# A range check moved behind the last eviction of its expert's first product, in twelve pieces over six experts

## The chip, the cores and the metric

One of the cores of a Trainium2 chip runs the whole kernel. A time is the microseconds that the chip takes for one execution. The kernel before took 680.99 us, the median of three runs (678.45 to 681.20).

The engines of the core work side by side, each through a queue of its own, in the order of that queue: TensorE (PE in the profile, its weight loads PEld) multiplies matrices into PSUM; VectorE (DVE), ScalarE (ACT) and GpSimd (POOL) work on tiles, GpSimd not on PSUM; SyncE (SP) issues most of the transfers. An instruction waits on semaphores until what it needs is there, and what stands behind it in its engine's queue waits with it.

## The reference

A gated recurrence feeds a mixture of experts. For every one of 4 x 8 heads and 768 steps of time, with complex gates a = a_re + i a_im of 48 channels:

```python
mag = np.sqrt(a_re * a_re + a_im * a_im)
scale = np.minimum(mag, 0.999) / (mag + 1e-06)
S = (a * scale)[..., None] * S + k[..., :, None] * v[..., None, :]     # complex state, 48 x 48
y = q @ S.real
```

The rows of all heads of a token, 384 numbers, are then x of 3072 tokens. Each token goes to the one of 8 experts that has its greatest logit:

```python
expert_idx = np.argmax(x @ w_gate, axis=1)
h = np.maximum(x_sorted[lo:hi] @ w1[e], 0.0)      # 384 -> 1024
y_sorted[lo:hi] = h @ w2[e]                       # 1024 -> 384
out = gate_w[:, None] * y[inv_perm]
```

## The kernel before

**Two stages.** The first stage (to about 330 us) computes the recurrence in chunks, routes the tokens and scatters their rows into a table in memory, sorted by expert. The second stage runs over the eight experts; the change is in it alone.

**An expert.** Each expert has room for CAP = 448 tokens, three tiles of 128 and one of 64 (expert 0 works in two parts). `gather` fetches its rows one expert ahead. `turn` transposes them on TensorE and copies the three parts of `xt` out of PSUM, the one in the middle on ScalarE (L78). In `expert` the first product goes over f = 0 to 7 (F = 1024 in eight parts): six matmuls a part into `hps`, which has three PSUM buffers, and a Relu into `ht`, on VectorE for even f (L589), on ScalarE for odd f (L587). The second product goes over the four tiles of tokens: 16 matmuls a tile into `yps`, which has two PSUM buffers; VectorE multiplies a full tile by the gate into `y` (L598); the short tile is put together from two halves by a copy on ScalarE (L605) and two operations on VectorE (L606, L607). GpSimd scatters each `y` to the output (L570). The second product reads all eight parts of `ht` for its first tile, and so can't get past the matmuls on f = 0 to 6 before the Relu of f = 7 is there.

**The weights.** `load_w(e + 2)` is written behind expert e: w1 (L162) goes out when the first product of e is over, w2 (L163) when the second is. Both are on SP's queue.

**The range check.** The first stage's method holds only for gates in a certain range. `range_check` therefore goes through all gates once more, in NC = 12 pieces of 128 x 768: it counts in `bad` where |a_im| exceeds 1.5 a_re or the square of the magnitude is under 0.37. A piece has two loads (L624), six operations on ScalarE (L626, L627, L629, L630, L632, L633, the last two with a sum into `bad`) and two on GpSimd (L628, L631), with two buffers for each of its four tiles. ScalarE and GpSimd take turns: the addition needs both Squares, the Copy overwrites what the addition read, the subtraction needs the Copy, the two Relus need the results of GpSimd. `verdict`, written behind expert 6, turns `bad` and the routing's overflow into `flag`: a sum on VectorE (L637 to L641), a matmul `bp`, a copy. If `flag` isn't zero, a slow version runs at the end; with these inputs it doesn't.

**What sets the order.** The text of the program gives priorities, and a planner writes each engine's queue: by a model of its own it simulates the engines, and at each moment takes the earliest written of the operations that it holds to be ready. `queue(ins, before)` ties an instruction behind another in that order, without a wait. The three pieces of each of e = 2 to 5 are written behind `load_w(e + 2)`, and so come to run in the first product of experts 3 to 6; their loads are tied behind the w2 load.

Of the kernel before, what the change touches and what calls it, by code (L numbers as in the profile page):

```python
# [10 lines left out]
FP = mybir.dt.float32  # L11
I32 = mybir.dt.int32
BF = mybir.dt.bfloat16
AF = mybir.ActivationFunctionType
# [6 lines left out]
P = 128  # L21
# [4 lines left out]
SLOPE = 1.5  # L26
# [11 lines left out]
def kernel(  # L38
# [12 lines left out]
    nc = tc.nc  # L51
# [4 lines left out]
    E, _, F = w1.shape  # L56
# [17 lines left out]
    def mm(o, lhsT, rhs, start=True, stop=True):  # L74
        return nc.tensor.matmul(o, lhsT=lhsT, rhs=rhs, start=start, stop=stop, skip_group_check=True)  # L75
# [10 lines left out]
    def const(shape, name, dt=FP):  # L86
        return cp.tile(shape, dt, name=name)
# [57 lines left out]
    T, W_T = {"put": []}, {}  # L145

    def queue(ins, before):

        tc.add_manual_dep(ins.ins, before.ins.name, NOSYNC, reason="queue order")
        return ins  # L150


    def load_w(e, parts=None):

        if e not in W_T:
            W_T[e] = [
                wp[e % 2].tile([P, n, w], FP, tag=nm, name=nm + "t") for nm, n, w in (("w1", KD, F), ("w2", KF, DM))
            ]
        a, b = W_T[e]
        w1e, w2e = w1[e].rearrange("(i p) f -> p i f", p=P), w2[e].rearrange("(i p) d -> p i d", p=P)  # L160
        if parts is None:
            nc.sync.dma_start(out=a, in_=w1e)  # L162
            T["w"] = nc.sync.dma_start(out=b, in_=w2e)  # L163
        else:
            for i in parts:
                o, x, i = (a, w1e, slice(i, i + 1)) if i < KD else (b, w2e, slice(2 * (i - KD), 2 * (i - KD) + 2))
                queue(nc.sync.dma_start(out=o[:, i], in_=x[:, i]), T["ld"])
# [307 lines left out]
    def gather(s, sizes):  # L475

        n = len(sizes)
        xg = gp.tile([P, n, XW], FP, tag="xg", padded_shape=[P, CT, XW], name="xg")
        f = sum(m == P for m in sizes)
        nc.sync.dma_start(out=xg[:, :f], in_=xs[s : s + f * P].rearrange("(i p) c -> p i c", p=P))  # L480
        if f < n:
            nc.sync.dma_start(out=xg[0 : sizes[f], f], in_=xs[s + f * P : s + f * P + sizes[f]])
        return xg
# [3 lines left out]
    for z in range(2):  # L487
        nc.sync.dma_start(
            out=wg[z * DP : z * DP + D, :, 0:E],
            in_=w_gate.rearrange("(i z d) e -> z d i e", z=2, d=D)[z],  # L490
# [59 lines left out]
    ck = ctx.enter_context(tc.tile_pool(name="ck", bufs=2))  # L550
# [4 lines left out]
    def turn(sizes, xg):  # L555
        n, w = len(sizes), sum(sizes)
        xt = xp.tile([P, KD, w], FP, tag="xt", padded_shape=[P, KD, CAP], name="xt")
        for d in range(KD):
            tp = psX.tile([P, w], FP, tag="tp", padded_shape=[P, 512], name="tp")
            for i, m in enumerate(sizes):  # L560
                nc.tensor.transpose(
                    out=tp[:, i * P : i * P + m],
                    in_=xg[0:m, i, d * P : (d + 1) * P],
                    identity=ident[0:m, 0:m],
                )
            copy(d, xt[:, d], tp)
        return xt

    def scatter(y, idx, m):
        return nc.gpsimd.indirect_dma_start(  # L570
            out=out,
            out_offset=bass.IndirectOffsetOnAxis(ap=idx, axis=0),
            in_=y[0:m],
            in_offset=None,
            bounds_check=N - 1,
            oob_is_err=False,
        )

    def expert(sizes, xt, wa, wb, xg):
        w = sum(sizes)  # L580
        ht = hp.tile([P, KF, w], FP, tag="ht", padded_shape=[P, KF, CAP], name="ht")
        for f in range(KF):
            ps = psH.tile([P, w], FP, tag="h", padded_shape=[P, 512], name="hps")
            for d in range(KD):
                mm(ps, wa[:, d, f * P : (f + 1) * P], xt[:, d], d == 0, d == KD - 1)
            if f % 2:
                nc.scalar.activation(out=ht[:, f], in_=ps, func=AF.Relu)  # L587
            else:
                nc.vector.tensor_scalar(out=ht[:, f], in0=ps, scalar1=0.0, scalar2=None, op0=OP.max)  # L589
        for i, m in enumerate(sizes):  # L590
            ps = psO.tile([P, DM], FP, tag="y", padded_shape=[P, 512], name="yps")
            y = yp.tile([P, DM], FP, tag="y", name="y")
            h = ht[:, :, i * P : i * P + m]
            gate = xg[0:m, i, DM : DM + 1]
            if m == P:
                for f in range(KF):
                    mm(ps, h[:, f], wb[:, f], f == 0, f == KF - 1)
                nc.vector.tensor_scalar(out=y, in0=ps, scalar1=gate, scalar2=None, op0=OP.mult)  # L598
            else:

                for f in range(KF // 2):
                    for z in range(2):
                        g = z * (KF // 2) + f
                        mm(ps[z * HT : (z + 1) * HT], h[:, g], wb[:, g], f == 0, f == KF // 2 - 1)
                nc.scalar.copy(out=y[0:m], in_=ps[HT : HT + m])  # L605
                nc.vector.tensor_tensor(out=y[0:m], in0=ps[0:m], in1=y[0:m], op=OP.add)  # L606
                nc.vector.tensor_scalar(out=y[0:m], in0=y[0:m], scalar1=gate, scalar2=None, op0=OP.mult)  # L607
            scatter(y, xg[0:m, i, DM + 1 : DM + 2].bitcast(I32), m)
# [3 lines left out]
    CW = 768  # L612
    NC = B * H * S * D // (P * CW)
    bad = const([P, 2, NC], "bad")
    mag2 = const([P, 1], "mag2")
    nc.vector.memset(mag2, MAG2_MIN)
    flat = [a.rearrange("b h s d -> (b h s d)").rearrange("(p n) -> p n", p=P) for a in (a_re, a_im)]

    def range_check(i):

        ar = ck.tile([P, CW], FP, tag="car", name="car")
        ai = ck.tile([P, CW], FP, tag="cai", name="cai")
        for t, a in zip((ar, ai), flat):
            queue(nc.sync.dma_start(out=t, in_=a[:, i * CW : (i + 1) * CW]), T["w"])  # L624
        s, w = [ck.tile([P, CW], FP, tag=nm, name=nm) for nm in ("cs", "cw")]
        nc.scalar.activation(out=s, in_=ar, func=AF.Square)  # L626
        nc.scalar.activation(out=w, in_=ai, func=AF.Square)  # L627
        nc.gpsimd.tensor_tensor(out=s, in0=s, in1=w, op=OP.add)  # L628
        nc.scalar.activation(out=ai, in_=ai, func=AF.Abs)  # L629
        nc.scalar.activation(out=w, in_=ar, func=AF.Copy, scale=SLOPE)  # L630
        nc.gpsimd.tensor_tensor(out=ai, in0=ai, in1=w, op=OP.subtract)  # L631
        nc.scalar.activation(out=ai, in_=ai, func=AF.Relu, accum_out=bad[:, 0, i : i + 1])  # L632
        nc.scalar.activation(out=s, in_=s, func=AF.Relu, scale=-1.0, bias=mag2, accum_out=bad[:, 1, i : i + 1])  # L633

    def verdict():

        nc.vector.tensor_scalar(out=bad, in0=bad, scalar1=0.0, scalar2=None, op0=OP.is_gt)  # L637
        two = xl.tile([P, 2], FP, tag="two", name="two")
        nc.vector.reduce_sum(two[:, 0:1], bad.rearrange("p a i -> p (a i)"), axis=AX_X)
        nc.vector.reduce_sum(two[:, 1:2], ov, axis=AX_X)  # L640
        nc.vector.tensor_tensor(out=two[:, 1:2], in0=two[:, 1:2], in1=two[:, 0:1], op=OP.add)  # L641
        bp = psX.tile([1, 2], FP, tag="tp", padded_shape=[1, 512], name="bp")
        mm(bp, ones[:, 0:1], two)
        nc.vector.tensor_copy(out=flag, in_=bp)
# [4 lines left out]
    for e in range(E):  # L649
        if e == 0:  # L650
            part = [([P] * (FIRST // P), own0), (rest0, gather(FIRST, rest0))]
        else:
            part = [(own, xg)]
        for i, (sizes, g) in enumerate(part):
            xt = turn(sizes, g)
            if i == len(part) - 1 and e + 1 < E:
                xg = gather((e + 1) * CAP, own)
            expert(sizes, xt, *W_T[e], g)
        if e + 2 < E:
            load_w(e + 2)  # L660
        if e >= 2:
            for i in range(NC):
                if i % (E - 4) == e - 2:
                    range_check(i)
        if e == E - 2:
            verdict()

# [151 lines left out]
```

## Time and profile before

| | |
|---|---|
| median of three runs | 680.99 us (678.45 to 681.20) |
| the profiled execution, its own time | 680.82 us |
| its span, first to last instruction | 678.8 us |
| mean granted clock of TensorE | 0.953 |
| TensorE matmuls busy | 591.6 us, 87% of the span |
| ScalarE busy | 276.0 us, 41% |
| VectorE busy | 238.3 us, 35% |
| GpSimd busy | 215.4 us, 32% |

The span runs from the first to the last instruction; the execution's own time has 2.0 us more around it. The granted clock is the share of full speed that the chip gave TensorE. Busy times of different engines overlap; idle time of an engine counts only where TensorE, or the end, waits for it.

### The profile page before, as it was taken

To read this page: it belongs to the slowest core of one execution; us is meant where nothing else is said; L and a number is where in the kernel's file an instruction comes from. 1 tells how busy PE (TensorE), PEld (TensorE's weight loads), DVE (VectorE), ACT (ScalarE), POOL (GpSimd) and SP (SyncE) were. 2 spreads that over 40 slices of the span, in tenths; PEclk is the share of its full clock that TensorE was granted. 3 is DMA by queue.
4 is the path that set the end of the run, shared out by engine and by line. 5 is a ranking of instruction groups with operands and counts; after the bars stand their busy time and mean duration, and the time that the engine had idled before them with its cause. 6 is when DMAs were issued, how large, how long until landed. Compare 5 with 4: busy or idle time off the path is not lost. (4 is left out here: it accounts for less than half of the span.)

```text
span 678.8 us, 8550 instructions
## 1 busy us (share of the span) xinstructions
PE 591.6 (87%) x3319; PEld 384.1 (57%) x3319; DVE 238.3 (35%) x487; ACT 276.0 (41%) x467; POOL 215.4 (32%) x206
## 2 busy tenths in 40 slices
PE   0497889897898899899999999997997997979993
PEld 0185667675776768677766555553553553535451
DVE  2453557566566547664312112120120210201210
ACT  4655765753863764663201101037054072270100
POOL 3543164254363462442121010125133143151001
PEclk9996799899899789899999999999997998997998
DMA  9999763753752641233126234364183362620000
GB/s 164 225 300 169 111 126 64 155 126 62 152 118 60 130 81 24 63 106 116 48 81 207 68 123 138 116 238 140 38 271 104 121 192 94 228 65 24 8 13 29
DMA packets 151673, 79.74 MB, mean 117 GB/s; under 512 B 130134, under 2 KB 141927, under 8 KB 151624
## 3 DMA queue, kind: packets, MB, share of 16 engines
q1 hardware_dynamic: 143168, 63.75, 39.8%
q0 software_dynamic: 4736, 15.20, 6.5%
q10 hardware_dynamic: 3720, 0.16, 0.3%
q8 instruction: 28, 0.46, 0.3%
q14 instruction: 21, 0.17, 0.1%
HBM read 63.74 MB, written 15.98 MB: 117 GB/s over the span
## 5 line engine op out<-in xcount | busy, mean ns | idle before, releaser
L75 PE MATMUL yps<-w2t,ht 128*128 128x384 f32 (+1 forms) x512 | 158.7, 510 | 17.4 <-ACT ht L587 17.2
L75 PE MATMUL hps<-xt,w1t 128*128 128x448 f32 (+2 forms) x432 | 147.0, 500 | 0.0
L75 PEld LDWEIGHTS yps<-w2t,ht 128*128 128x128 f32 (+1 forms) x512 | 85.3, 186 | 89.1 <-issue 24.2
L75 PEld LDWEIGHTS hps<-xt,w1t 128*128 128x128 f32 x432 | 79.9, 190 | 61.6 <-issue 58.2
L570 POOL DMA_INDIRECT out_dram<-y,xg x32 | 30.8, 961 | 199.7 <-DVE y L598 163.8
L75 PE MATMUL at<-qt,kt 96*128 96x128 f32 x384 | 58.5, 300 | 17.1 <-ACT kt L78 9.3
L75 PEld LDWEIGHTS at<-qt,kt 96*128 96x128 f32 x384 | 51.8, 208 | 28.0 <-ACT kt L78 12.8
L598 DVE TENSOR_SCALAR y<-yps,xg 128x384 f32<-128x384 f32 x24 | 14.8, 617 | 145.2 <-PE yps L75 145.2
L589 DVE TENSOR_SCALAR ht<-hps 128x448 f32<-128x448 f32 (+2 forms) x36 | 20.6, 572 | 102.4 <-PE hps L75 102.4
L605 ACT COPY y<-yps 64x384 f32<-64x384 f32 x8 | 3.8, 476 | 126.3 <-PE yps L75 126.3
L587 ACT ACTIVATE ht<-hps 128x448 f32<-128x448 f32 (+2 forms) x36 | 17.8, 495 | 87.3 <-PE hps L75 87.3
L75 PE MATMUL y<-am,v 128*64 128x128 f32 x384 | 51.0, 299 | 0.0
L320 POOL TENSOR_TENSOR Qe<-q,E 128x384 f32<-128x384 f32 x24 | 23.9, 998 | 84.6 <-ACT E L185 84.5
L424 DVE TENSOR_TENSOR am<-at,tri 128x512 f32<-128x512 f32 x48 | 33.0, 688 | 37.5 <-PE at L75 37.4
L75 PE MATMUL csl<-A,tri_half 128*128 128x384 f32 x48 | 25.4, 616 | 21.1 <-DVE A L238 18.5
L75 PE MATMUL y<-qt,G 96*64 96x128 f32 x320 | 42.2, 281 | 0.0
L391 POOL DMA_INDIRECT xs<-x,to x24 | 24.3, 1013 | 55.9 <-DMA xs<-x,to 36.6
L416 PE MATMUL tp<-ident,Q 128*96 128x128 f32 x192 | 35.0, 304 | 3.7 <-DVE Q L324 3.7
L75 PEld LDWEIGHTS y<-am,v 128*64 128x64 f32 x384 | 31.2, 144 | 10.1 <-issue 6.9
L75 PE MATMUL dk<-v,K 128*96 128x48 f32 x320 | 34.1, 260 | 2.8 <-DVE t L454 2.8
L191 ACT ACT_TABLE_LOAD x27 | 34.6, 1283 | 2.3 <-PEq L805 0.8
L75 PEld LDWEIGHTS dk<-v,K 128*96 128x96 f32 x320 | 32.4, 177 | 5.0 <-DVE t L454 4.0
(124 smaller groups left out, 816.6 us busy)
## 6 DMA issues: line engine op xcount, KB each, us to landing
w1t<-in_moe_w_dram SPq DMA_DIRECT2D x7, 1536.0 KB
w2t<-in_moe_w_dram SPq DMA_DIRECT2D x7, 1536.0 KB
xs<-zrow POOLq DMA_DIRECT2D x1, 5404.0 KB, 23.7
ar<-in_a_re_dram SPq DMA_DIRECT2D x12, 384.0 KB
ai<-in_a_im_dram SPq DMA_DIRECT2D x12, 384.0 KB
q<-in_q_dram SPq DMA_DIRECT2D x12, 384.0 KB
k<-in_k_dram SPq DMA_DIRECT2D x12, 384.0 KB
v<-in_v_dram SPq DMA_DIRECT2D x12, 384.0 KB
```

The lines of the kernel that those rows point to most:

```text
L75: return nc.tensor.matmul(o, lhsT=lhsT, rhs=rhs, start=start, stop=stop, skip_group_check=True)
L191: ins = nc.scalar.preload_act_table_set(name)
L320: T[nm] = nc.gpsimd.tensor_tensor(out=e.rearrange("p h d -> p (h d)"), in0=T[src, u][:, sl], in1=T[dec, u][:, sl], op=OP.mult)
L391: return nc.gpsimd.indirect_dma_start(out=xs[:, :], out_offset=bass.IndirectOffsetOnAxis(ap=to[:, i : i + 1], axis=0), in_=x[:, i], in_off ...
L416: nc.tensor.transpose(out=tp[0:DD, j], in_=X[:, hg * 4 + j], identity=ident)
L424: nc.vector.tensor_tensor(out=am, in0=at, in1=bc(tri, 1, 4), op=OP.mult)
L570: return nc.gpsimd.indirect_dma_start(out=out, out_offset=bass.IndirectOffsetOnAxis(ap=idx, axis=0), in_=y[0:m], in_offset=None, bounds_ch ...
L587: nc.scalar.activation(out=ht[:, f], in_=ps, func=AF.Relu)
L589: nc.vector.tensor_scalar(out=ht[:, f], in0=ps, scalar1=0.0, scalar2=None, op0=OP.max)
L598: nc.vector.tensor_scalar(out=y, in0=ps, scalar1=gate, scalar2=None, op0=OP.mult)
L605: nc.scalar.copy(out=y[0:m], in_=ps[HT : HT + m])
```

## The change

The pieces of the range check are dealt out in pairs to experts 1 to 6, in place of three pieces to each of four. `range_check` is split in two. `range_load` issues a piece's two loads and is written where the check was, at the end of expert e (0 to 5). The operations themselves are handed to the next expert in `beside`, and written between its first and its second product. Every operation on ScalarE is tied in ScalarE's order: the first behind the Relu of f = 7, each behind the one before it, and the Relu of f = 1 of the following expert behind the last of the pair. The last two Relus of a piece have changed places. `verdict` stays where it was.

```diff
-    def expert(sizes, xt, wa, wb, xg):
+    def expert(sizes, xt, wa, wb, xg, beside=()):
...
             if f % 2:
-                nc.scalar.activation(out=ht[:, f], in_=ps, func=AF.Relu)
+                relu = nc.scalar.activation(out=ht[:, f], in_=ps, func=AF.Relu)
+                if T.get("beside"):
+                    queue(relu, T.pop("beside"))
             else:
                 nc.vector.tensor_scalar(out=ht[:, f], in0=ps, scalar1=0.0, scalar2=None, op0=OP.max)
+        for f in beside:
+            relu = T["beside"] = f(relu)
...
-    def range_check(i):
-
-        ar = ck.tile([P, CW], FP, tag="car", name="car")
-        ai = ck.tile([P, CW], FP, tag="cai", name="cai")
-        for t, a in zip((ar, ai), flat):
-            queue(nc.sync.dma_start(out=t, in_=a[:, i * CW : (i + 1) * CW]), T["w"])
+    def range_load(i):
+        t = [ck.tile([P, CW], FP, tag=nm, name=nm) for nm in ("car", "cai")]
+        for o, a in zip(t, flat):
+            queue(nc.sync.dma_start(out=o, in_=a[:, i * CW : (i + 1) * CW]), T["w"])
+        T["ck", i] = t
+
+    def range_check(i, before):
+
+        ar, ai = T.pop(("ck", i))
         s, w = [ck.tile([P, CW], FP, tag=nm, name=nm) for nm in ("cs", "cw")]
-        nc.scalar.activation(out=s, in_=ar, func=AF.Square)
-        nc.scalar.activation(out=w, in_=ai, func=AF.Square)
+
+        def on_act(**kw):
+            nonlocal before
+            before = queue(nc.scalar.activation(**kw), before)
+
+        on_act(out=s, in_=ar, func=AF.Square)
+        on_act(out=w, in_=ai, func=AF.Square)
         nc.gpsimd.tensor_tensor(out=s, in0=s, in1=w, op=OP.add)
-        nc.scalar.activation(out=ai, in_=ai, func=AF.Abs)
-        nc.scalar.activation(out=w, in_=ar, func=AF.Copy, scale=SLOPE)
+        on_act(out=ai, in_=ai, func=AF.Abs)
+        on_act(out=w, in_=ar, func=AF.Copy, scale=SLOPE)
         nc.gpsimd.tensor_tensor(out=ai, in0=ai, in1=w, op=OP.subtract)
-        nc.scalar.activation(out=ai, in_=ai, func=AF.Relu, accum_out=bad[:, 0, i : i + 1])
-        nc.scalar.activation(out=s, in_=s, func=AF.Relu, scale=-1.0, bias=mag2, accum_out=bad[:, 1, i : i + 1])
+        on_act(out=s, in_=s, func=AF.Relu, scale=-1.0, bias=mag2, accum_out=bad[:, 1, i : i + 1])
+        on_act(out=ai, in_=ai, func=AF.Relu, accum_out=bad[:, 0, i : i + 1])
+        return before
...
-            expert(sizes, xt, *W_T[e], g)
+            todo = []
+            if i == len(part) - 1 and 1 <= e < E - 1:
+                todo = [lambda b, i=i: range_check(i, b) for i in range(NC) if i % (E - 2) == e - 1]
+            expert(sizes, xt, *W_T[e], g, todo)
         if e + 2 < E:
             load_w(e + 2)
-        if e >= 2:
-            for i in range(NC):
-                if i % (E - 4) == e - 2:
-                    range_check(i)
+        for i in range(NC):
+            if i % (E - 2) == e:
+                range_load(i)
         if e == E - 2:
             verdict()
```

## Rows read from the trace of the kernel before

**Rows 1.** Waits from 380 to 680 us: total, times, longest.

```profile
PE yps L75 <- ACT ht L587: 17.2, 6, 4.1
```

**Rows 2.** Busy time by stretch: experts 1 and 3 to 6 (us, engines, clock, DMA).

```profile
368.40:407.00 38.60, 38.56 (x126) 20.56 (x124) 6.37 (x11) 3.18 (x6) 3.86 (x4) 1.00 0.35 114
445.61:490.43 44.82, 40.73 (x126) 21.20 (x125) 6.37 (x11) 17.85 (x30) 14.71 (x10) 0.96 0.45 152
490.43:536.79 46.36, 42.13 (x127) 21.89 (x125) 6.37 (x11) 17.85 (x30) 14.69 (x10) 0.93 0.45 147
536.79:582.03 45.24, 40.79 (x126) 21.17 (x125) 6.37 (x11) 17.85 (x30) 14.71 (x10) 0.96 0.45 150
582.03:629.05 47.02, 42.27 (x128) 22.00 (x126) 6.89 (x14) 17.85 (x30) 14.71 (x10) 0.93 0.35 114
```

**Rows 3.** The same: second products of experts 1 and 3, expert 4 after its stop.

```profile
388.70:407.00 18.30, 18.30 (x65) 9.99 (x63) 1.85 (x3) 0.54 (x1) 2.93 (x3) 1.00 0.31 111
465.90:490.43 24.53, 20.47 (x65) 10.63 (x64) 1.85 (x3) 6.69 (x12) 7.02 (x6) 0.93 0.22 83
...
519.86:536.79 16.93, 16.93 (x51) 8.94 (x51) 1.85 (x3) 0.00 (x0) 2.93 (x3) 0.82 0.07 28
```

**Rows 4.** Timeline of TensorE, experts 3 and 4: start, length, what.

```profile
474.91 15.59 PE L75 MATMUL yps<-w2t,ht 128*128 128x384 f32 x50 [4.06 <-ACT ht L587]
...
519.86 16.99 PE L75 MATMUL yps<-w2t,ht 128*128 128x384 f32 x50 [4.05 <-ACT ht L587]
```

**Rows 5.** Timeline of ScalarE in expert 3.

```profile
454.52 0.84 ACT L627 ACTIVATE cw<-cai 128x768 f32<-128x768 f32 x1 [0.28 <-DMA cai<-in_a_im_dram]
...
461.63 0.52 ACT L587 ACTIVATE ht<-hps 128x448 f32<-128x448 f32 x1
...
467.25 0.82 ACT L626 ACTIVATE cs<-car 128x768 f32<-128x768 f32 x1
...
468.72 0.52 ACT L587 ACTIVATE ht<-hps 128x448 f32<-128x448 f32 x1
...
473.49 0.84 ACT L632 ACTIVATE cai<-cai 128x768 f32<-128x768 f32 x1 [0.99 <-POOL cai L631]
...
474.33 0.52 ACT L587 ACTIVATE ht<-hps 128x448 f32<-128x448 f32 x1
```

**Rows 6.** Timeline of ScalarE from expert 1 to expert 2.

```profile
384.39 0.54 ACT L587 ACTIVATE ht<-hps 128x448 f32<-128x448 f32 x1 [3.97 <-PE hps L75]
388.90 0.54 ACT L587 ACTIVATE ht<-hps 128x448 f32<-128x448 f32 x1 [3.97 <-PE hps L75]
407.12 0.48 ACT L605 COPY y<-yps 64x384 f32<-64x384 f32 x1 [17.68 <-PE yps L75]
408.53 0.53 ACT L78 COPY xt<-tp 128x448 f32<-128x448 f32 x1 [0.94 <-PE tp L561]
```

**Rows 7.** Timeline of GpSimd, experts 1 and 3.

```profile
394.95 0.98 POOL L570 DMA_INDIRECT out_dram<-y,xg  x1 [22.15 <-DVE y L598]
400.11 0.98 POOL L570 DMA_INDIRECT out_dram<-y,xg  x1 [4.18 <-DVE y L598]
405.27 0.98 POOL L570 DMA_INDIRECT out_dram<-y,xg  x1 [4.19 <-DVE y L598]
...
468.89 1.82 POOL L628 TENSOR_TENSOR cs<-cs,cw 128x768 f32<-128x768 f32 x1 [2.51 <-ACT cw L627]
471.66 1.80 POOL L631 TENSOR_TENSOR cai<-cai,cw 128x768 f32<-128x768 f32 x1 [0.95 <-ACT cw L630]
```

**Rows 8.** Timeline of SP's queue in expert 3.

```profile
446.19 0.52 SPq L624 DMA_DIRECT2D car<-in_a_re_dram  x1
...
454.53 0.38 SPq L480 DMA_DIRECT2D xg<-xs  x1
```

**Rows 9.** Timeline of VectorE, experts 1 and 6.

```profile
399.22 0.62 DVE L598 TENSOR_SCALAR y<-yps,xg 128x384 f32<-128x384 f32 x1 [4.54 <-PE yps L75]
...
611.54 0.18 DVE L637 TENSOR_SCALAR bad<-bad 128x24 f32<-128x24 f32 x1 [10.65 <-ACT cai L632]
```

## The prediction

> **What bounds the kernel now.** I read the page first: TensorE is by far the busiest engine, so only what makes TensorE idle or slow can be won. Then the waits, cut to the expert stage: the largest wait of TensorE there is on ScalarE's Relu of `ht`, 17.2 us in six waits [rows 1]; the longer waits in that view belong to engines waiting for TensorE. Then busy time by stretch, one stretch for each expert. Experts 1 and 2 take 38.6 us at a granted clock of 1.00, experts 3 to 6 take 44.82, 46.36, 45.24 and 47.02 us at 0.93 to 0.96 [rows 2]. The four that are long are the four with range-check work on ScalarE (17.85 us busy against 3.18) and GpSimd. Their excess over 38.60 is 6.22 + 7.76 + 6.64 + 8.42 = 29.0 us.
>
> Where in an expert is it? The second product alone takes 18.30 us in expert 1 and 24.53 us in expert 3, 6.23 more, which is the whole excess of that expert [rows 3]; the turn and the first product cost nothing extra, even with the checks and their loads beside them. The timelines show the mechanism. In expert 3 TensorE stops for 4.06 us before its 15th matmul of the second product until `ht` comes [rows 4], and `ht` is late because the Relu of f = 7 stands in ScalarE's queue behind the last operation of the third piece: that operation starts at 473.49 us, the Relu at 474.33 us [rows 5], although the first product ended at 465.90 us. [...]
>
> **The change, part by part.** *The order.* The checks now start behind Relu f = 7 of their own expert, so no Relu of the first product can stand behind them. That removes the stops and with them what slows the clock: -29.0 us, if nothing new stands in their place. What hides the checks is the second product: 18.30 us in which ScalarE has one 0.54 us Relu at the start and then nothing until the copy of the short tile at 407.12 us [rows 6].
>
> *Does a pair fit?* One piece in the new order (two Squares, Abs, Copy after the addition, two Relus) took, as piece three of expert 3, from 467.25 us to the next instruction at 474.33 us: 7.08 us, with GpSimd's addition (1.82 us) and subtraction inside it; the Relu that stood within hid in the wait for the addition [rows 5, 7]. The swap of the two last Relus only writes down the order that ScalarE already had. Two pieces are 14.16 us. In expert 1 Relu f = 7 runs from 388.90 to 389.44 us, so the chain ends at about 403.6 us. The first thing behind it on ScalarE is the copy that can't start before 407.12 us: 3.5 us of slack. After that comes the copy of `xt` from 408.53 to 409.06 us, which the next first product waits for. So per expert the cost is nothing, covered by the second product; if the cover were gone, each us over the 3.5 would hold that copy and then TensorE.
>
> The rule that nothing overtakes on ScalarE is what cost the time before: the Relu of f = 7 waited 8 us behind check work [rows 5]. [...]
>
> *GpSimd.* It now has four tensor operations of about 1.81 us between the scatters of the same product [rows 7]. In the piece just shown the addition began 1.64 us after the first Square and the subtraction 4.41 us after it [rows 5, 7]. With the first Square 0.54 us behind the start of Relu f = 7, and counted from that start, ScalarE asks for add 1 at +2.2 us, subtract 1 at +4.95, add 2 at +9.3, subtract 2 at +12.0; the scatters come free at +6.05, +11.21 and +16.37 us (394.95, 400.11, 405.27 us) and take 0.98 us [rows 7]. In that order of time only the second scatter touches the chain: it ends at +12.19, which costs subtract 2 about 0.2 us. The trace of before doesn't show the new order on GpSimd. The bounds: nothing if the order follows the real times; 2.1 to 2.9 us, still within the slack, if the first scatter stands ahead of subtract 1 and the second ahead of add 2. I take nothing. What hints at the order that the planner will choose is the one it chose before: one Relu of the first product (461.63, 468.72 us) to each piece, though in fact a piece takes 7.08 us and the Relus are 4.5 us apart [rows 5, 6]. So it believed a piece to be shorter against TensorE's work than it is, and will put the checks' operations early, ahead of the scatters, which is the harmless side.
>
> *The loads.* They move one expert ahead of their use, still behind w2's load on SP's queue. At expert 3 they were issued from 446.19 us and the first pair had landed by 454.52 us [rows 5, 8]; issued right behind the end of the expert before, as there, a pair has until Relu f = 7, some 20 us after that end. The gather queued behind them comes 8 us after the first of them [rows 8]. There is no third pair any more that waits for a buffer in the middle of an expert; the buffers of a pair are free at 403.6 us, before the w2 load at the expert's end. Expert 3's first product, in which such loads landed, lost nothing (above), so I cost them at zero.
>
> *Experts 1 and 2* now carry a pair too: zero by the same sum.
>
> *The verdict.* It now waits for the second piece of expert 6. Before, `bad` stood in VectorE's queue 10.65 us waiting for its last piece, ahead of the first eviction [rows 9]. If it is planned between the first and second eviction of expert 6, the second (399.22 us in expert 1's times) waits until 403.6 + 0.6 for the verdict's operations and ends at about 404.8; with two `yps` buffers the fourth tile, which starts when the third is done (404.4, 5.16 us behind the second by their scatters), is held some 0.5 us. Planned later it costs nothing; planned ahead of the first eviction, the third tile is held some 6 us, and with the clock loss of the stops above 8 to 10 us. I take 0.5.
>
> **Sum.** Profiled execution 680.8 us (span 678.8 and 2.0 around it; the median of three runs is 681.0, so the same). 680.8 - 29.0 + 0.5 = 652.3 us.
>
> **Rivals.**
> 1. *A chain held on GpSimd, middle size.* If the second scatter (ends +12.19) stands ahead of subtract 1, that ends at +14.0, piece two begins 0.87 us later, as the next instruction did after the subtraction of the piece shown [rows 5, 7], and ScalarE is free at +22.0, 410.9 us. Two copies of 0.5 us later, at 411.9 us, `xt` is there, 2.8 us after the 409.06 of before: 2.8 us in each of six experts, and 2.2 more where the clock falls: 652 + 17 to 30 = 669 to 682 us. For it: the four operations and three scatters do share one queue. Against: the planner's early checks. Chance 0.05.
> 2. *Slower than before.* The same mechanism one scatter further decides: with the third (ends +17.35) ahead of subtract 1, everything is 5.2 us later again, and TensorE loses 8.0 us and 2.2 to 3.7 of clock (what the stops of experts 3 and 4 cost beyond their length) in each of six experts: 61 to 70 us, some 715 us. It turns slower than before when the loss per expert passes 29 / 6 = 4.8 us. Against it: the third scatter comes free 11 us after that subtraction is asked for. Chance 0.03.
> 3. *The change moves the stall, no gain.* If the chain's ends are so late that the next expert's first Relu, tied behind them, is held as f = 7 was, the 29 us come back in another place: 677 to 684 us. With three `hps` buffers the product stops first at f = 4, half its 18 us after it began, which is when the `xt` copy ends at 409.06 us, so ScalarE would have to be late with f = 1 until 418 us, 14 us after the chain's end by my sum. Against: just that distance. Chance 0.04.
> 4. *The verdict ahead of the first eviction*: 652 + 8 to 10 = 660 to 662 us, with smaller mishaps at the seams between 655 and 660. Chance 0.10.
>
> **How the numbers follow.** The forecast has 0.78 and its own range is 650 to 655 us. The three runs shown lie between 678.45 and 681.2, so I let the low end go to 649.5; the high end takes in most of the fourth rival, to 660. Left out are the rest of rival 4 and rivals 1 to 3, under 2 in 10. Half a per cent, 3.4 us, is about what a measurement of this kernel can tell from no change. Faster: the forecast, rival 4 and most of rival 1, 0.92; same: rival 3 and the top of rival 1, 0.04; slower: rival 2 and a rest, 0.04.
>
> **What would show it.** Right: experts 1 to 6 each within 0.3 us of 38.6 us and at clock 1.00; no wait of TensorE for ScalarE's `ht`; six chains that each begin within 0.6 us of a Relu of f = 7, the pair about 14.2 us later; the copy of the short tile following TensorE at once, and the scatters within a microsecond of their evictions. Wrong: a gap before the first product on the copy of `xt`, GpSimd's tensor operations waiting behind scatters, a range-check load still on its way when the chain begins, or `bad` holding an eviction for more than a tile.

## The result, and the profile after

The changed kernel takes 651.35 us (median of four runs, 650.07 to 655.58) against 679.72 us for the kernel before (four runs, 675.53 to 681.20): a ratio of 0.9603, 95% interval 0.9539 to 0.9667. The forecast was 652.3 us in a range of 649.5 to 660. The profiled execution took 650.52 us, its span is 648.5 us.

Busy time by stretch, one row for each of experts 1 to 7, as in [rows 2] (us of the stretch; busy time and instructions of TensorE, its weight loads, VectorE, ScalarE, GpSimd; granted clock; DMA share; GB/s):

```profile
367.18:405.79 38.61, 38.58 (x127) 20.56 (x125) 6.38 (x11) 13.19 (x22) 10.99 (x8) 1.00 0.45 153
405.79:444.38 38.59, 38.55 (x126) 20.56 (x124) 6.38 (x11) 13.19 (x22) 11.09 (x9) 1.00 0.45 157
444.38:482.99 38.61, 38.58 (x127) 20.57 (x125) 6.38 (x11) 13.19 (x22) 11.12 (x9) 1.00 0.46 156
482.99:521.58 38.59, 38.55 (x126) 20.56 (x124) 6.38 (x11) 13.19 (x22) 11.11 (x9) 1.00 0.45 156
521.58:560.19 38.61, 38.58 (x127) 20.57 (x125) 6.38 (x11) 13.18 (x22) 11.10 (x9) 1.00 0.44 156
560.19:599.25 39.06, 38.74 (x128) 20.64 (x126) 6.62 (x14) 13.19 (x22) 10.28 (x8) 1.00 0.33 115
599.25:637.90 38.65, 38.03 (x124) 20.55 (x124) 6.53 (x12) 3.18 (x6) 4.80 (x5) 1.00 0.04 15
```

Experts 1 to 5 each take 38.6 us at a clock of 1.00, though ScalarE now works 13.2 us in each of them. Only expert 6, with the verdict, is 0.46 us longer. Against [rows 2] experts 3 to 6 give back 6.21 + 7.77 + 6.63 + 7.96 = 28.6 us. The rest of the difference between the two profiled executions, 30.3 us, is 1.2 us ahead of expert 1, which begins at 367.18 us instead of 368.40 behind the first stage and expert 0, whose work the change doesn't touch, and 0.5 us behind expert 6.

ScalarE in expert 1, its timeline around the pair (start, length, what, idle time ahead of it and what ended that):

```profile
387.68 0.54 ACT L588 ACTIVATE ht<-hps 128x448 f32<-128x448 f32 x1 [3.97 <-PE hps L75]
388.12 0.83 ACT L637 ACTIVATE cs<-car 128x768 f32<-128x768 f32 x1
...
395.22 0.83 ACT L637 ACTIVATE cs<-car 128x768 f32<-128x768 f32 x1
...
402.21 0.19 ACT L637 ACTIVATION_READ_ACCUMULATOR cai<-cai 128x1 f32 x1
405.90 0.47 ACT L610 COPY y<-yps 64x384 f32<-64x384 f32 x1 [3.50 <-PE yps L75]
407.25 0.53 ACT L78 COPY xt<-tp 128x448 f32<-128x448 f32 x1 [0.88 <-PE tp L561]
```

The answer to [rows 6]: the Relu of f = 7 starts when TensorE has finished its product, the first piece follows 0.44 us later, the second 7.10 us after that, and the pair ends at 402.40 us. Then ScalarE is idle 3.50 us until TensorE ends: the slack of the forecast, 3.5 us.

GpSimd in expert 1, its timeline:

```profile
389.77 1.81 POOL L641 TENSOR_TENSOR cs<-cs,cw 128x768 f32<-128x768 f32 x1 [18.18 <-ACT cw L637]
392.53 1.81 POOL L644 TENSOR_TENSOR cai<-cai,cw 128x768 f32<-128x768 f32 x1 [0.95 <-ACT cw L637]
394.49 1.00 POOL L570 DMA_INDIRECT out_dram<-y,xg  x1 [0.15 <-issue]
396.87 1.80 POOL L641 TENSOR_TENSOR cs<-cs,cw 128x768 f32<-128x768 f32 x1 [1.38 <-ACT cw L637]
399.62 1.81 POOL L644 TENSOR_TENSOR cai<-cai,cw 128x768 f32<-128x768 f32 x1 [0.95 <-ACT cw L637]
401.59 0.99 POOL L570 DMA_INDIRECT out_dram<-y,xg  x1 [0.16 <-issue]
```

All six pairs show this order: the first two scatters of an expert each stand behind a subtraction, and no scatter stands ahead of an operation of the pair that was wanted at that time. The second scatter is 3 us late, its `y` having been ready at 398.62 us; nothing waits for it.

At the verdict, VectorE and TensorE in expert 6 (two timelines):

```profile
595.43 0.18 DVE L651 TENSOR_SCALAR bad<-bad 128x24 f32<-128x24 f32 x1 [8.97 <-ACT cai L637]
595.64 0.18 DVE L653 TENSOR_REDUCE two<-bad 128x1 f32<-128x24 f32 x1
595.74 0.61 DVE L603 TENSOR_SCALAR y<-yps,xg 128x384 f32<-128x384 f32 x1
...
596.40 2.80 PE L75 MATMUL yps<-w2t,ht 128*64 128x384 f32 x16 [0.28 <-DVE y L603]
```

`bad` stands between the first and the second eviction of expert 6 and holds the second until 595.74 us; TensorE stops 0.28 us before its last tile.

### The profile page after: what moved, and what is told of

Read it like the earlier page. It is cut to its first block, busy times and chain, and to the rows that moved or that the text cites. A ratio compares the mean times of both kernels' runs of the same rounds, so it can differ in the third digit from the quotient of the medians.

```text
span 648.5 us, 8554 instructions
## 1 busy us (share of the span) xinstructions
PE 577.9 (89%) x3319; PEld 378.7 (58%) x3319; DVE 238.3 (37%) x487; ACT 277.8 (43%) x467; POOL 215.0 (33%) x206
## 5 line engine op out<-in xcount | busy, mean ns | idle before, releaser
L75 PE MATMUL yps<-w2t,ht 128*128 128x384 f32 (+1 forms) x512 | 147.2, 488 | 0.3 <-DVE y L603 0.3
L75 PEld LDWEIGHTS yps<-w2t,ht 128*128 128x128 f32 (+1 forms) x512 | 81.4, 177 | 64.5 <-issue 15.0
L75 PE MATMUL at<-qt,kt 96*128 96x128 f32 x384 | 57.1, 295 | 18.1 <-ACT qt L78 9.4
L75 PEld LDWEIGHTS at<-qt,kt 96*128 96x128 f32 x384 | 50.3, 203 | 28.8 <-ACT qt L78 12.9
L641 POOL TENSOR_TENSOR cs<-cs,cw 128x768 f32<-128x768 f32 x12 | 21.6, 1804 | 117.4 <-ACT cw L637 117.4
L75 PE MATMUL y<-am,v 128*64 128x128 f32 x384 | 49.1, 288 | 0.0
L78 ACT COPY qt<-tp 96x512 f32<-96x512 f32 x48 | 27.0, 581 | 20.1 <-PE tp L416 18.8
```

The costliest lines, as they stand in the source:

```text
L78: (nc.scalar.copy if i % 2 else nc.vector.tensor_copy)(out=o, in_=in_)
```

## Experiments

Totals of these kernels also hold the first stage and expert 0, whose code none of them touches and which took 364.6 to 371.5 us in their profiled executions. So the table gives two things: all runs, and in the profiled execution the time from the start of expert 1's transposes to the end of the span.

| kernel | median us | ratio to before (95%) | span less start of expert 1, us |
|---|---|---|---|
| before | 679.72 | 1 | 678.8 - 368.40 = 310.4 |
| changed | 651.35 | 0.960 (0.954 to 0.967) | 648.5 - 367.18 = 281.3 |
| spread alone | 649.97 | 0.958 (0.950 to 0.967) | 647.4 - 365.95 = 281.5 |
| place alone | 667.17 | 0.985 (0.978 to 0.993) | 662.7 - 365.80 = 296.9 |
| no tie | 651.66 | 0.962 (0.954 to 0.970) | 650.1 - 368.98 = 281.1 |
| no check | 654.53 | 0.962 (0.952 to 0.971) | 653.0 - 371.51 = 281.5 |
| four a time | 685.32 | 1.012 (1.006 to 1.019) | 683.1 - 368.36 = 314.7 |
| subtractions behind a scatter | 673.32 | 0.992 (0.988 to 0.996) | 671.6 - 366.85 = 304.8 |
| two, then one | 648.35 | 0.958 (0.954 to 0.962) | 645.8 - 364.61 = 281.2 |
| verdict later | 651.65 | 0.961 (0.955 to 0.966) | 649.2 - 367.87 = 281.3 |

The ratios are to the runs of the kernel before on the same chip as each kernel; the medians of the first two rows are those given above.

**1. The dealing alone.** The forecast took the new place for what removes the stops. The first run, an edit of the kernel before, does without it.

```diff
-        if e >= 2:
-            for i in range(NC):
-                if i % (E - 4) == e - 2:
-                    range_check(i)
+        for i in range(NC):
+            if i % (E - 2) == e:
+                range_check(i)
```

> The kernel before with one edit: a pair of pieces to each of experts 1 to 6 in place of three pieces to each of four; nothing is tied, loads and operations stay where they were written, so the checks run in the first product. Theory: what cost 29 us was the third piece, since only Relu f = 7 behind it came too late; with two pieces of 7.1 us from some 5 us into the first product on, Relu f = 7 can follow less than 2 us after its product, and the second product needs it only some 4.6 us after that product's end. So 651 to 653 us, no wait of TensorE for ht. Rival (the place behind f = 7 and the tie make the gain): Relus f = 5 and f = 7 are still held behind check work, TensorE still stops, now in six experts, and the time is over 660 us.

Measured: 649.97 us, and 281.5 us from expert 1 on: the whole gain. ScalarE in expert 3, its timeline:

```profile
450.99 0.84 ACT L626 ACTIVATE cs<-car 128x768 f32<-128x768 f32 x1 [0.33 <-DMA car<-in_a_re_dram]
...
459.32 0.52 ACT L587 ACTIVATE ht<-hps 128x448 f32<-128x448 f32 x1
...
464.10 0.84 ACT L632 ACTIVATE cai<-cai 128x768 f32<-128x768 f32 x1 [1.00 <-POOL cai L631]
464.85 0.19 ACT L632 ACTIVATION_READ_ACCUMULATOR cai<-cai 128x1 f32 x1
464.94 0.95 ACT L587 ACTIVATE ht<-hps 128x448 f32<-128x448 f32 x2
```

The pair runs in the middle of the first product and holds the Relus of f = 3 and f = 5, the latter until 464.94 us. Both last Relus are then done at 465.89 us, 2.4 us after the second product began at 463.45 us, and TensorE's rows show no stop. In [rows 5] the Relu of f = 7 started 8.4 us after that point. What cost the time before was the third piece ahead of it.

**2. The place alone.** The changed kernel with three pieces to each of experts 3 to 6.

```diff
-        t = [ck.tile([P, CW], FP, tag=nm, name=nm) for nm in ("car", "cai")]
+        t = [ck.tile([P, CW], FP, tag=nm, name=nm, bufs=3) for nm in ("car", "cai")]
...
-        s, w = [ck.tile([P, CW], FP, tag=nm, name=nm) for nm in ("cs", "cw")]
+        s, w = [ck.tile([P, CW], FP, tag=nm, name=nm, bufs=1) for nm in ("cs", "cw")]
...
-            if i == len(part) - 1 and 1 <= e < E - 1:
-                todo = [lambda b, i=i: range_check(i, b) for i in range(NC) if i % (E - 2) == e - 1]
+            if i == len(part) - 1 and 3 <= e < E - 1:
+                todo = [lambda b, i=i: range_check(i, b) for i in range(NC) if i % (E - 4) == e - 3]
...
-            if i % (E - 2) == e:
+            if i % (E - 4) == e - 2:
                 range_load(i)
```

> The changed kernel with the old dealing: three pieces to each of experts 3 to 6, loaded one expert ahead (three buffers for each of the two loaded tiles, one for each of the two others so that they fit), tied behind Relu f = 7 as in the change. Theory: the chain is 21.3 us where some 17.8 are free, so the copy of the short tile is some 3.5 us late and the middle part of xt some 2.6 us; TensorE waits 1.8 to 2.6 us at the start of four first products, plus up to 2.2 us each where the clock falls: 651 + 7 to 19 = 658 to 670 us. Rival (the place alone makes the gain, the number of pieces doesn't matter): 650 to 653 us.

Measured: 667.17 us, 15.6 us more from expert 1 on than the change (296.9 - 281.3). ScalarE, then TensorE, at the seam from expert 3 to expert 4 (two timelines):

```profile
485.14 0.19 ACT L637 ACTIVATION_READ_ACCUMULATOR cai<-cai 128x1 f32 x1
485.35 0.48 ACT L610 COPY y<-yps 64x384 f32<-64x384 f32 x1
485.86 0.53 ACT L78 COPY xt<-tp 128x448 f32<-128x448 f32 x1
...
486.44 17.56 PE L75 MATMUL hps<-xt,w1t 128*128 128x448 f32 x46 [1.67 <-ACT xt L78]
```

The chain takes 21.4 us (463.93 to 485.33 us) and ends 3.7 us after the second product; the two copies follow without a gap, and the first product of expert 4 stops 1.67 us before its third matmul. Three seams have that stop; at the last, after expert 6, the verdict's matmul waits 4.42 us for VectorE's sums, which wait for the last piece. These waits are 9.4 of the 15.6 us. Most of the rest is TensorE's own pace: behind the second of the three stops the first product goes on for 18.95 us at a granted 0.92, behind the other two for 17.39 us at 1.00, and the 48 matmuls of expert 7's first product take 20.83 us instead of 18.14.

**3. Without the tie.** The changed kernel, all else as it is.

```diff
-                if T.get("beside"):
-                    queue(relu, T.pop("beside"))
...
-            before = queue(nc.scalar.activation(**kw), before)
+            before = nc.scalar.activation(**kw)
```

> The changed kernel without the ties in ScalarE's order; loads one expert ahead, operations written at the same place between the products, pairs over six experts. The planner then mixes the checks into the first product, with Relu f = 7 behind the pair's last operation. Theory: a pair begun behind f = 1 and held up by f = 3 and f = 5 still ends some 1.5 us after the first product, Relu f = 7 comes some 3 us before it is needed, no stop: 650 to 653 us, as the change. Rival (the tie is what makes the gain): stops of TensorE on ht come back in six experts, 655 us or more.

Measured: 651.66 us, 281.1 us from expert 1 on. The planner does move the checks into the first product. ScalarE, then TensorE, in expert 1 (two timelines):

```profile
390.94 0.52 ACT L588 ACTIVATE ht<-hps 128x448 f32<-128x448 f32 x1
...
389.27 18.38 PE L75 MATMUL yps<-w2t,ht 128*128 128x384 f32 x64
```

The Relu of f = 7 starts at 390.94 us, 1.67 us after the second product began at 389.27 us, which is early enough: TensorE runs its 64 matmuls without a stop. With pairs, the tie is worth nothing here.

**4. Without the check.**

```diff
+    nc.vector.memset(bad, 0.0)
...
-            if i == len(part) - 1 and 1 <= e < E - 1:
-                todo = [lambda b, i=i: range_check(i, b) for i in range(NC) if i % (E - 2) == e - 1]
...
-        for i in range(NC):
-            if i % (E - 2) == e:
-                range_load(i)
```

> The changed kernel without the range check: no loads of the gates for it, none of its operations; bad is set to zero, the verdict still runs. It leaves that part of the work out. Theory: the twelve pieces now cost only the 0.5 us at the verdict of expert 6, so this is at most 1 us faster than the changed kernel: 650 to 651 us, each expert 38.6 us. Rival (the pairs still cost something that the trace does not show as a wait, by the loads, by GpSimd beside VectorE or by the clock): 648 us or less.

Measured: 281.5 us from expert 1 on, against 281.3 with the check. The median of the runs, 654.53 us (646.84 to 655.24), lies over the expected 650 to 651: in the profiled execution expert 1 began only at 371.51 us, and the code ahead of it is the same in all. So the twelve pieces now cost nothing that the time from expert 1 on shows. What they do cost is seen in expert 6, with the verdict: 39.06 us with them, 38.72 without. The end of the span, which differs by half a microsecond among these kernels (run 8), covers that up.

**5. Four a time.** As run 2, with four pieces to each of experts 4 to 6: four buffers for `car` and `cai`, `E - 5` for the dealing, `TS = 8` in the slow version, which doesn't run, for room.

```diff
-                todo = [lambda b, i=i: range_check(i, b) for i in range(NC) if i % (E - 2) == e - 1]
+                todo = [lambda b, i=i: range_check(i, b) for i in range(NC) if i % (E - 5) == e - 4]
```

> The changed kernel with four pieces to each of experts 4, 5 and 6 (four buffers for each of the two loaded tiles, one for each of the two others; a smaller step of time in the slow version, which doesn't run, makes the room), tied behind Relu f = 7. Theory: place and tie are the change's, but the chain is 28.4 us and ends 9.7 us after xt is wanted; two seams between experts lose 8.8 us and 2.2 to 3.7 of clock each, the third some 12 and 2 to 4 because the verdict waits for the last piece too: 651 + 36 to 41 = 687 to 692 us, slower than the kernel before although no Relu is ever late. Rival (behind f = 7 checks are hidden whatever their number): 655 us or less.

Measured: 685.32 us, slower than before by 1.2%. TensorE's timeline, at the seam after expert 4 and after expert 6:

```profile
534.66 18.86 PE L75 MATMUL hps<-xt,w1t 128*128 128x448 f32 x44 [7.97 <-ACT xt L78]
...
631.55 0.19 PE L75 MATMUL bp<-two,ones 128*1 128x2 f32 x2 [11.46 <-DVE two L655]
```

No Relu is late in this kernel; the copy of `xt` is. The loss is 314.7 - 281.3 = 33.4 us where 36 to 41 were expected: the stops at the copy are 8.0 instead of 8.8 us, and at each seam the transposes and matmuls behind the stop took only some 1.5 to 2.6 us longer than at the pace of experts without a stop (18.70 and 18.14 us for 44 matmuls that take 16.63 at that pace, 22.88 us for the transposes and the first product of expert 7 instead of 20.30).

**6. The bad order on GpSimd.** The changed kernel, its subtractions tied behind the second scatter.

```diff
-        for f in beside:
-            relu = T["beside"] = f(relu)
...
-            scatter(y, xg[0:m, i, DM + 1 : DM + 2].bitcast(I32), m)
+            sc = scatter(y, xg[0:m, i, DM + 1 : DM + 2].bitcast(I32), m)
+            if beside and i == 1:
+                for f in beside:
+                    relu = T["beside"] = f(relu, sc)
...
-        nc.gpsimd.tensor_tensor(out=ai, in0=ai, in1=w, op=OP.subtract)
+        queue(nc.gpsimd.tensor_tensor(out=ai, in0=ai, in1=w, op=OP.subtract), sc)
```

> The changed kernel with the order on GpSimd made the bad one: the two subtractions of a pair are tied behind the second scatter of their expert (the pair is written behind that scatter; ScalarE's order, the pairs and the loads are the change's). Theory: subtraction one starts 7 us late, at about +12.2 us from Relu f = 7, the chain ends at +22 us, the middle part of xt is 3 us late and TensorE loses 2.3 to 4 us at five seams and 6 to 7 at the last, where the verdict waits: 651 + 18 to 27 = 669 to 678 us. Rival (GpSimd's order doesn't matter, there is room): 650 to 655 us.

Measured: 673.32 us. GpSimd, then ScalarE, in expert 1 (two timelines):

```profile
398.56 0.97 POOL L570 DMA_INDIRECT out_dram<-y,xg  x1 [4.16 <-DVE y L601]
399.55 1.82 POOL L645 TENSOR_TENSOR cai<-cai,cw 128x768 f32<-128x768 f32 x1
...
401.40 0.84 ACT L638 ACTIVATE cai<-cai 128x768 f32<-128x768 f32 x1 [8.37 <-POOL cai L645]
...
410.18 0.53 ACT L78 COPY xt<-tp 128x448 f32<-128x448 f32 x1
```

The Copy that the subtraction needs was done near 392 us; the subtraction waits for the scatter, which waits for VectorE, which waits for TensorE's second tile. ScalarE stands idle 8.37 us in the middle of its chain, and the copy of `xt` ends 3.3 us later after the Relu of f = 7 than in the change (23.37 against 20.10 us). That is the forecast's first rival, which it gave 669 to 682 us. It was real as a mechanism and didn't come about, because the planner put the operations ahead.

**7. Two, then one.** The old dealing, with only the third piece behind the Relu of f = 7 of experts 3 to 6 (three buffers for `car` and `cai`, `TS = 8`).

```diff
-            before = queue(nc.scalar.activation(**kw), before)
+            ins = nc.scalar.activation(**kw)
+            if before is not None:
+                before = queue(ins, before)
...
-                todo = [lambda b, i=i: range_check(i, b) for i in range(NC) if i % (E - 2) == e - 1]
+                todo = [lambda b: range_check(e + 5, b)]
...
-            if i % (E - 2) == e:
+            if i % (E - 4) == e - 2:
                 range_load(i)
+                if i < 8:
+                    range_check(i, None)
```

> The old dealing, three pieces to each of experts 3 to 6, with only the third one moved: two run untied in the first product as before, the third is tied behind Relu f = 7 and runs in the second product (three buffers for the loaded tiles, room made as in the run with four pieces). Theory: neither the dealing over six experts nor the place of the checks counts, only that Relu f = 7 isn't behind a third piece: 650 to 653 us, no stop of TensorE. Rival (at most two pieces per expert can be hidden): 658 us or more.

Measured: 648.35 us, 281.2 us from expert 1 on. ScalarE in expert 3, its timeline:

```profile
463.32 0.18 ACT L637 ACTIVATION_READ_ACCUMULATOR cai<-cai 128x1 f32 x1
463.41 0.96 ACT L588 ACTIVATE ht<-hps 128x448 f32<-128x448 f32 x2
464.26 0.84 ACT L637 ACTIVATE cs<-car 128x768 f32<-128x768 f32 x1
...
480.52 0.47 ACT L610 COPY y<-yps 64x384 f32<-64x384 f32 x1 [9.06 <-PE yps L75]
```

Three pieces in an expert hide as well as two, once the last of them isn't ahead of the Relu: 9.06 us of ScalarE are still free before the seam.

**8. The verdict later.** The first two lines stand in `expert`, between the products.

```diff
+        if T.get("verdict"):
+            T.pop("verdict")()
...
         if e == E - 2:
-            verdict()
+            T["verdict"] = verdict
```

> The changed kernel with the verdict written between the two products of expert 7 in place of the end of expert 6. Theory: the seam between experts 6 and 7 loses the verdict's matmul and the wait of the transposes for ScalarE's copy, 0.6 to 0.8 us; the 0.3 us stop before the last tile of expert 6 stays, since the sums on VectorE stay where they were planned. 650.5 us, which the runs can't tell from the change, but the trace can. Rival (the end of the kernel then waits for the flag): 1 us or more slower, seen behind the last scatter.

Measured: 651.65 us, 281.3 us from expert 1 on, as the change. TensorE in expert 7, its timeline:

```profile
599.82 2.22 PE L561 MATMUL tp<-ident,xg 128*128 128x128 f32 x12
601.97 18.31 PE L75 MATMUL hps<-xt,w1t 128*128 128x448 f32 x48
620.21 0.19 PE L75 MATMUL bp<-two,ones 128*1 128x2 f32 x2
620.33 18.48 PE L75 MATMUL yps<-w2t,ht 128*128 128x384 f32 x64
```

The seam itself is shorter, the transposes of expert 7 and their wait take 2.15 us (599.82 to 601.97) instead of 2.74. But the matmul `bp` now stands between the two products of expert 7, which begin 18.36 us apart instead of 18.14, and from the start of that last second product to the end of the span 28.9 us pass instead of 28.4. That need not be the verdict's doing: in the kernels that leave the verdict where it was, the same stretch takes 28.4 to 28.9 us (28.9 in the kernel before, 28.8 in runs 1 and 4). Behind the last scatter the span goes on for 7.2 to 7.3 us in the change and here, so the end doesn't wait for the flag, as the rival had it. Why this stretch differs among the kernels isn't settled.

## Why the prediction was right, step by step

**The bound.** It held in the main: the excess of experts 3 to 6 stood behind late Relus, and with these in time experts 3 to 5 take 38.6 us and expert 6 39.06 us, at a clock of 1.00 as in experts 1 and 2. Two details were off. Two of the six waits in [rows 1] aren't for the Relu of f = 7 but, four matmuls earlier, for that of f = 5, which was held by check work too (TensorE in experts 5 and 6 of the kernel before, its timeline):

```profile
560.83 1.56 PE L75 MATMUL yps<-w2t,ht 128*128 128x384 f32 x4 [0.36 <-ACT ht L587]
...
606.38 1.56 PE L75 MATMUL yps<-w2t,ht 128*128 128x384 f32 x4 [0.66 <-ACT ht L587]
```

And the 2.2 to 3.7 us of clock with which the rivals priced a stop were too many. In an expert without a stop the 15th matmul of the second product begins about 4.5 us after the first (14 of the 16 matmuls of a tile, which take 5.16 us), and 13.8 of the 18.3 us remain. In experts 3 to 6 it began 9.0 to 9.7 us after the first, which is a delay of 19.1 us in all four; from there the product took 15.5 to 16.9 us, 9.8 us too much in all. The stretch behind the stop of expert 3:

```profile
474.91:490.43 15.52, 15.52 (x50) 8.23 (x51) 1.85 (x3) 0.00 (x0) 2.93 (x3) 0.89 0.08 30
```

So the product behind a stop took 1.7 to 3.1 us longer than without one, at a granted 0.89 in experts 3 and 5 and 0.82 in experts 4 and 6; the rest of the excess is delay ahead of the 15th matmul. The sum isn't touched: with the stops gone experts 3 to 6 run at 1.00.

**The order.** The step said that the checks start behind the Relu of f = 7 and that this removes the stops. That is what the changed kernel does, but the attribution was too narrow. The place isn't needed (runs 1 and 3), and with three pieces it isn't enough: it moves the stop to the copy of `xt` (run 2). What removes the stops is that not more than two pieces stand ahead of the Relu of f = 7; the dealing does that by itself, and so does moving one piece in three (run 7). The numbers for it were in [rows 5] before: the second piece was over by 467.25 us, 1.35 us after the first product.

**Does a pair fit.** 14.16 us forecast, 14.28 measured (388.12 to 402.40 us), slack 3.5 and 3.50 us. Runs 2 and 5 show what lies beyond the slack: 1.67 us of stop for a chain one piece longer, 7.97 for two.

**GpSimd.** The planner put the operations early, as its one Relu to each piece had suggested, and the chain wasn't held. Only the scatters are later than "within a microsecond": the second by 3 us, the first and third by 1.0 and 1.2, at no cost. Run 6 shows that the harmless order was worth some 22 us (23.5 us from expert 1 on). In it a subtraction stands behind a scatter on GpSimd and waits for nothing but its place: it starts 7.0 us later than in the change, 399.55 less 392.53 us, in executions whose Relu of f = 7 starts 0.34 us apart.

**The loads and experts 1 and 2.** Zero, as taken: their rows are those of the others, and leaving the check out altogether (run 4) gives 281.5 us, no less.

**The verdict.** The place was right, between the first and the second eviction of expert 6. The stop was 0.28 us instead of 0.5, and the matmul `bp` at the seam makes up most of the rest of expert 6's 0.46, which is over the 0.3 us that the forecast allowed an expert.

**The sum.** 310.4 - 29.0 + 0.5 = 281.9 us from expert 1 to the end of the span, measured 281.3; the remaining 1.2 us to the profiled execution came from the time ahead of expert 1. That the median of the runs lies within 1 us of 652.3 is partly luck, since that time differs by up to 7 us among the profiled executions of these kernels.

**Rivals.** The third didn't arise. The first and the mechanism of the second are real: run 6 is the first at its full size, and run 5 reached the far side of no gain by a longer chain. The fourth didn't come about, as `bad` stood behind the first eviction.

## What to carry to other kernels

ScalarE, busy 41% of the span before, held TensorE, busy 87%, for 17.2 us by what stood ahead of Relus of 0.52 us in its queue. So look for the instruction on which the bottleneck waits, count how much side work may run ahead of it before it is late, and deal the side work in portions under that; where exactly they then stand mattered little here (281.1 to 281.5 us from expert 1 on in the change and in runs 1, 3 and 7). The tie that fixes the place only moved the deadline to the next instruction that the bottleneck needs, here the copy of `xt`, which starts 19 us after the pair (407.25 less 388.12 us) and with three pieces stops TensorE for 1.67 us (run 2): work out the chain against that deadline, with every engine that it passes through.

## What the runs showed that had not been expected

The same stop doesn't always cost the same. In run 6 five seams have a stop of 2.15 to 2.17 us. Busy time by stretch, from the stop to the end of the first product, for the first and the last two of them:

```profile
410.76:428.16 17.40, 17.39 (x47) 8.85 (x48) 3.33 (x6) 1.63 (x3) 0.92 (x1) 1.00 0.45 166
...
533.84:552.93 19.09, 19.09 (x46) 9.41 (x47) 3.33 (x6) 1.63 (x3) 0.92 (x1) 0.91 0.40 147
576.58:595.45 18.87, 18.87 (x46) 9.49 (x47) 3.33 (x6) 1.63 (x3) 0.92 (x1) 0.92 0.42 152
```

The same 46 matmuls (the first row also counts one at its edge) take 17.4 us at a granted clock of 1.00 after three of the stops and 18.9 to 19.1 us at 0.91 to 0.92 after two. Run 2 shows the same: after its second stop of 1.67 us the clock fell, after the first and third it didn't. What decides is not shown by these runs.

And the first stage with expert 0, the same code in every kernel here, ended between 364.6 and 371.5 us in the profiled executions. That is more than any difference among the kernels without a stop at a Relu or at the copy of `xt`, which lie within 281.1 and 281.5 us from expert 1 on. Where a change touches one stage, that stage's own time in the trace tells apart what the medians of the runs can't.
